# The second expert product with one 80-column stationary operand per chunk in place of a 64-column and a 16-column one

## The chip, the cores and the metric

The kernel runs on one core of one Trainium2 chip. The metric is device time in microseconds, the median of several executions. TensorE (PE, and PEld for its weight loads), VectorE (DVE), ScalarE (ACT) and GpSimd (POOL) each take their instructions in order; SyncE (SP) issues the large transfers.

## What is computed

A gated recurrence over 4 sequences of 5056 steps and 256 channels, then a mixture of 8 experts on the 20224 resulting rows. Each row goes to the expert with the largest logit, and each expert keeps the 80 rows with the largest gate; all other output rows are zero.

```python
for t in range(S):
    h = f[:, t] * h + i[:, t] * x[:, t]
    y[:, t] = h
...
for e in range(E):
    ...
    h = np.maximum(x[tok_idx] @ w1[e], 0.0)
    out[tok_idx] = gate_w[tok_idx, None] * (h @ w2[e])
```

`w1[e]` is 256 x 1024, `w2[e]` is 1024 x 256, all in fp32.

## The kernel before

The first part computes the recurrence in transposed form (channels on partitions) into `h_all`, 40 units of 512 steps, and the gate logits; then a ranking stage finds the 80 rows of each expert. The last part, `experts`, is where the change lies.

Per expert e it has these steps. `gather(e)` (L719) copies 80 columns of `h_all` into X(e), 24 on VectorE, 32 on ScalarE and 24 on GpSimd, each of which first loads the column numbers into registers; `scaled(e)` (L730) multiplies X(e) on GpSimd. `hidden(e)` (L736), the first product, called h(e) below, multiplies the 80 rows by `w1[e]`: the stationary operand is a piece of 64 columns of `w1`, the moving one is X(e) with 80 columns, and two pieces go to the two halves of the PSUM partitions. `relu(e)` (L753) rectifies the lower half of the 1024 hidden channels on ScalarE and the upper half on VectorE, into HID(e), eight chunks of 128 channels x 80 rows. `result(e)` (L757), the second product, called y(e) below, goes over the eight chunks: HID is stationary, `w2` moves with 256 columns, and the 80 rows are cut into two pieces, rows 0 to 63 and rows 64 to 79. `finish(e)` (L767) multiplies by the gates on VectorE, and `scatter(e)` (L773) writes the 80 rows to the output by an indirect transfer of GpSimd.

The order is written out by hand: h(0), h(1), then for each e the rectification of e, h(e+1) if it is still to come, the gather of e+3, y(e), the finish of e. So TensorE runs h(0), h(1), y(0), h(2), y(1), h(3), ..., h(7), y(6), y(7), with seven warm-up matmuls (L160, 128 stationary columns, 512 moving) around h(0) and h(1). After y(0) VectorE works out the output rows of all experts (L834 to L837, `rows_of`) before its half of relu(1).

The weights come in halves of 512 KB: two per `w1[e]` and two per `w2[e]`, in the list `w1[0]`, `w1[1]`, `w2[0]`, `w1[2]`, `w2[1]`, `w1[3]`, `w2[2]`, `w1[4]`, `w2[3]`, `w1[5]`, `w2[4]` and so on (L505). Seven slots hold them in turn, so half k can be loaded when TensorE is through with half k - 7. SyncE issues them in this order; between them it issues copies that clear parts of the output (`copied`, L131, 512 KB each, the last one 256 KB), after the halves with the numbers in

```python
BETWEEN = (7, 8, 8, 10, 12, 13, 15, 16, 18)
```

(L526). Of the list's numbers, 11 is the second half of `w1[3]`, 12 the first half of `w2[2]` and 20 the first half of `w2[4]`. A DMA queue of SyncE has eight semaphores, and a transfer waits until the one eight before it has landed.

The scatters of experts 2 to 6 wait for a mark on TensorE, a given chunk of a given second product (`apart`, L814; for expert 6 it is chunk 6 of y(7)), and the scatter of expert 7 waits until all others have landed.

Of the kernel before, what the change touches and what calls it, by code (L numbers as in the profile page):

```python
# [26 lines left out]
def kernel(  # L27
# [11 lines left out]
    nc = tc.nc  # L39
# [4 lines left out]
    FC = F // P  # L44
# [5 lines left out]
    K = (capacity + TOP - 1) // TOP * TOP  # L50
# [20 lines left out]
    FH, CH = F // 2, FC // 2  # L71
# [90 lines left out]
    with tc.tile_pool(name="gsm", bufs=1) as gsm:  # L162
# [239 lines left out]
        with tc.tile_pool(name="plg", bufs=1, space=PSUM) as plg, \  # L402
# [48 lines left out]
            with tc.tile_pool(name="pct", bufs=4, space=PSUM) as pct:  # L451
                cts = {}

                def turn(*runs):
                    ct = pct.tile([P, 4 * P], F32, name="ct", tag="ct")
                    for g0, g1 in runs:
                        turned(ct[:, ds((g0 - runs[0][0]) * P, (g1 - g0) * P)], g0, g1)
                        cts[g0] = ct, runs[0][0]
                    return ct
# [24 lines left out]
                c = turn((6, LAST - 1), (LAST - 1, LAST))  # L484
# [113 lines left out]
    with tc.tile_pool(name="sel", bufs=1) as sel, \  # L598
# [17 lines left out]
        for r in (rivals2, rivals):  # L616
            nc.tensor.matmul(r, mates, spread.rearrange("p c k -> p (c k)"),
                             start=True, stop=True)
# [89 lines left out]
    def experts(again):  # L708
        with tc.tile_pool(name="xp", bufs=3) as xp, \
# [7 lines left out]
            sent, marks = [], {}  # L717
# [16 lines left out]
            H = P // 2  # L734
# [22 lines left out]
            def result(e):  # L757
                halves = [w.pop((2, e, i)) for i in range(2)]
                hid = HID.pop(e)
                y = Y[e] = psy.tile([K, D], F32, name="y_ps", tag="y_ps")  # L760
                for c in range(FC):
                    for s0, n in ((0, H), (H, K - H)):
                        marks[e, c] = nc.tensor.matmul(  # L763
                            y[ds(s0, n)], hid[:, c, ds(s0, n)], halves[c // CH][:, c % CH],
                            start=c == 0, stop=c == FC - 1, skip_group_check=True)

            def finish(e):  # L767
                if e == 0:
# [47 lines left out]
            for e in range(E):  # L816
                relu(e, ps)
                if e == 0 and not again:
                    gates_of(slots[:, 1])
                if e + 1 < E:  # L820
                    ps = hidden(e + 1)
                    more(1)
                if e == E - 4:
                    scatter(0)
                if e + 3 < E:
                    gather(e + 3)
                    scaled(e + 3)
                if e == E - 4:
                    scatter(1)
                result(e)  # L830
                more(1)
                finish(e)
                if e == 0 and not again:
                    found = consts.tile([1, 1], F32, name="found")  # L834
                    nc.vector.tensor_reduce(found, total, AX.X, ALU.add)
                    nc.vector.tensor_copy(doubt, found)
                    rows_of(consts, slots[:, 0], slots[:, 1])  # L837
# [94 lines left out]
```

## Time and profile before

| | us |
|---|---|
| median of 3 runs (252.64 to 252.92) | 252.69 |
| the profiled execution | 253.41 |
| its span, first to last instruction | 251.5 |
| TensorE busy, of that span | 221.4 (88%) |
| VectorE, ScalarE, GpSimd busy | 156.8, 133.1, 143.2 |

Times in the trace count from the start of the span. A busy matmul record is a pipelined one: records overlap, and the distance between the starts of two records tells the cost of the first. An fp32 matmul stands in the trace as two records, each with a weight load of its own.

### The profile page before, as it was taken

The page shows a single profiled execution, that of the slowest core. Times are in us where ns is not written, and L with a number is a line of the kernel's source. Part 1 is how long each engine was busy: PE and PEld are TensorE (multiplying, and loading weights), DVE is VectorE, ACT ScalarE, POOL GpSimd, SP SyncE. Part 2 cuts the span into 40 slices and gives each one's busy share as a digit, 9 for nine tenths or more (in the row PEclk, how much of TensorE's full clock was granted, in tenths as well). Part 3 has the DMA queues.
Part 4 walks back from the last instruction along what each step waited for, and adds up shares of the span by engine and source line. Part 5 has one row for each costly group of instructions (what it writes and reads, how often), then busy time and mean ns, then how long its engine had stood idle before and what let it go on. Part 6 is the DMA issues. An engine that isn't in the chain of part 4 may idle for free.

```text
span 251.5 us, 6853 instructions
## 1 busy us (share of the span) xinstructions
PE 221.4 (88%) x2223; PEld 141.9 (56%) x2223; DVE 156.8 (62%) x400; ACT 133.1 (53%) x419; POOL 143.2 (57%) x287
## 2 busy tenths in 40 slices
PE   0699899899989998999966899799999999999960
PEld 0698787778868787777834646252525344352210
DVE  4189699999999999899999567435415051010100
ACT  4488798779787886888826066755042300000000
POOL 4678797889788798779844067650450620011211
PEclk9999999999999999999997979999999999999996
DMA  6999999999999999999999999969985474620000
GB/s 248 377 410 449 371 425 412 418 420 401 412 405 408 397 434 391 395 403 412 400 363 417 416 444 402 417 257 345 340 300 199 154 250 137 219 95 14 26 20 17
DMA packets 21363, 80.61 MB, mean 320 GB/s; under 512 B 2580, under 2 KB 2710, under 8 KB 20888
## 3 DMA queue, kind: packets, MB, share of 16 engines
q1 hardware_dynamic: 20936, 79.45, 80.4%
q0 software_dynamic: 384, 0.66, 0.9%
q8 instruction: 19, 0.31, 0.5%
q14 instruction: 24, 0.20, 0.2%
HBM read 72.62 MB, written 21.36 MB: 374 GB/s over the span
## 4 chain that ended last, share of the span: by engine, by line
PE 45%; issue 19%; ACT 10%; DVE 9%; DMA 9%; POOL 4%; ACTq 1%; DVEq 0%; POOLq 0%; SPq 0%
PE y_ps L763 14%; PE sp L251 11%; PE up L259 9%; PE lg L289 6%; DMA x_t<-in_x_dram 5%; ACT h_all L268 4%; ACT xe L727 3%; PE h_ps L747 3%; DMA f_t<-in_f_logit_dram 3%; DVE h_all L276 3%; POOL out_dram L775 2%; PE lt L313 2%; POOL x_t L245 2%; ACT ls L298 2%; DMA out_dram<-y,goal 1%
## 5 line engine op out<-in xcount | busy, mean ns | idle before, releaser
L245 POOL TENSOR_TENSOR x_t<-f_t,x_t 128x1024 f32<-128x1024 f32 x40 | 94.7, 2370 | 21.1 <-DMA x_t<-in_x_dram 10.6
L276 DVE TENSOR_TENSOR_SCAN h_all<-h_all,up 128x512 f32<-128x512 f32 (+1 forms) x80 | 95.8, 1244 | 9.9 <-PE up L259 6.4
L763 PE MATMUL y_ps<-w_sb,hid 128*64 128x256 f32 (+1 forms) x256 | 71.3, 393 | 1.4 <-ACT hid L754 1.4
L268 ACT ACTIVATE h_all<-sp,nomlb 128x512 f32<-128x512 f32 (+1 forms) x80 | 50.3, 677 | 16.5 <-PE sp L251 15.7
L763 PEld LDWEIGHTS y_ps<-w_sb,hid 128*64 128x64 f32 (+1 forms) x256 | 19.4, 115 | 50.4 <-issue 48.8
L241 ACT ACTIVATE f_t<-f_t 128x1024 f32<-128x1024 f32 x40 | 42.3, 1058 | 9.8 <-DMA f_t<-in_f_logit_dram 7.3
L259 PE MATMUL up<-ident,x_t 128*128 128x128 f32 x320 | 44.0, 278 | 2.8 <-DVE h_all L276 2.2
L251 PE MATMUL sp<-ident,f_t 128*128 128x128 f32 x320 | 45.4, 287 | 0.0
L251 PEld LDWEIGHTS sp<-ident,f_t 128*128 128x128 f32 x320 | 35.9, 145 | 7.8 <-issue 7.1
L259 PEld LDWEIGHTS up<-ident,x_t 128*128 128x128 f32 x320 | 36.7, 143 | 5.1 <-DVE h_all L276 3.7
L771 DVE TENSOR_SCALAR y<-y_ps,gates 80x256 f32<-80x256 f32 x8 | 3.8, 480 | 57.0 <-PE y_ps L763 51.5
L727 ACT COPY xe<-h_all 128x2 f32 x256 | 25.4, 190 | 18.8 <-issue 12.2
L727 POOL COPY xe<-h_all 128x2 f32 x192 | 24.3, 189 | 14.2 <-issue 7.0
L727 DVE COPY xe<-h_all 128x2 f32 x192 | 22.7, 173 | 12.0 <-issue 7.4
L775 POOL DMA_INDIRECT out_dram<-y,goal x8 | 7.5, 942 | 35.3 <-PE y_ps L763 31.1
L289 PE MATMUL lg<-h_all,wg 128*32 128x128 f32 (+1 forms) x640 | 26.4, 282 | 0.6 <-ACT ls L298 0.6
L754 ACT ACTIVATE hid<-h_ps 128x320 f32<-128x320 f32 x8 | 3.5, 435 | 39.2 <-PE h_ps L747 21.3
L747 PEld LDWEIGHTS h_ps<-xe,w_sb 128*64 128x64 f32 x512 | 18.2, 138 | 4.1 <-issue 3.6
L747 PE MATMUL h_ps<-xe,w_sb 128*64 128x80 f32 x512 | 19.5, 234 | 0.0
L289 PEld LDWEIGHTS lg<-h_all,wg 128*32 128x32 f32 x640 | 15.4, 108 | 7.0 <-issue 4.9
L731 POOL TENSOR_TENSOR xe<-xe,omlb 128x160 f32<-128x160 f32 x8 | 3.6, 452 | 23.5 <-DVE xe L727 22.1
L160 PE MATMUL warm<-h_all,ident 128*128 128x512 f32 x22 | 13.1, 740 | 0.0
(128 smaller groups left out, 105.6 us busy)
## 6 DMA issues: line engine op xcount, KB each, us to landing
f_t<-in_f_logit_dram SPq DMA_DIRECT2D x40, 512.0 KB, 6.6
x_t<-in_x_dram SPq DMA_DIRECT2D x40, 512.0 KB, 6.9
w_sb<-in_moe_w_dram SPq DMA_DIRECT2D x31, 512.0 KB, 5.0
out_dram<-out_dram SPq DMA_DIRECT2D x26, 512.0 KB, 8.2
out_dram<-zbuf SPq DMA_DIRECT2D x12, 512.0 KB, 10.0
out_dram<-h_all SPq DMA_DIRECT2D x1, 512.0 KB, 8.2
w_sb<-in_moe_w_dram SPq DMA_DIRECT2D x2, 256.0 KB, 2.8
out_dram<-out_dram SPq DMA_DIRECT2D x1, 256.0 KB
```

The lines of the kernel that those rows point to most:

```text
L160: nc.tensor.matmul(warm, ident, h_all[:, 0, :4 * P], start=True, stop=True)
L241: nc.scalar.activation(s_t, s_t, ACT.Sigmoid, scale=-1.0)
L245: nc.gpsimd.tensor_tensor(u_t, sts[n], u_t, ALU.mult)
L251: nc.tensor.transpose(ps[:, ds(r * P, P)], sts[n][:, r, ds(o * P, P)], ident)
L259: nc.tensor.transpose(ps[:, r::R], uts[n][:, r, ds(o * P, P)], ident)
L268: nc.scalar.activation(columns(n, o).rearrange("p (k r) -> p k r", r=R), sps.pop((n, o)).rearrange("p (r k) -> p k r", r=R)[:, P - run(n / ...
L276: nc.vector.tensor_tensor_scan(h, h, ups.pop((n, o)), h_all[:, o, ds(spot(n - B) + G - 1, 1)] if n >= B else 0.0, ALU.mult, ALU.add)
L289: nc.tensor.matmul(lgs[g][ds(q * LC, LC), b, :k].rearrange("p (m i) -> p m i", i=2), wg[:, o], pairs[:, :, q], start=o == 0, stop=o == DC ...
L727: copy(X[e][:, :, ds(k + j, 1)], h_all[:, :, ds(v, 1)])
L747: nc.tensor.matmul(ps[i][ds(s * H, H), c], wo[o][:, at:at + J * (H - 1) + 1:J], xt[:, o], start=o == 0 and c == 0, stop=o == DC - 1, skip_ ...
L763: marks[e, c] = nc.tensor.matmul(y[ds(s0, n)], hid[:, c, ds(s0, n)], halves[c // CH][:, c % CH], start=c == 0, stop=c == FC - 1, skip_grou ...
L775: sent.append(nc.gpsimd.indirect_dma_start(out=out, out_offset=bass.IndirectOffsetOnAxis(ap=goal[:, ds(e, 1)], axis=0), in_=rows.pop(e), i ...
```

## The change

`result` runs one matmul per chunk, with all 80 columns of the chunk of HID as the stationary operand, and writes the whole `y` tile with it. The mark of a chunk is that matmul.

```diff
@@ -759,10 +759,9 @@
                 hid = HID.pop(e)
                 y = Y[e] = psy.tile([K, D], F32, name="y_ps", tag="y_ps")
                 for c in range(FC):
-                    for s0, n in ((0, H), (H, K - H)):
-                        marks[e, c] = nc.tensor.matmul(
-                            y[ds(s0, n)], hid[:, c, ds(s0, n)], halves[c // CH][:, c % CH],
-                            start=c == 0, stop=c == FC - 1, skip_group_check=True)
+                    marks[e, c] = nc.tensor.matmul(
+                        y, hid[:, c], halves[c // CH][:, c % CH],
+                        start=c == 0, stop=c == FC - 1, skip_group_check=True)
```

On TensorE, from the end of h(1) through y(0) to h(2), the program before has, with the waits of each instruction (DMAHW is a landing of weights; the sizes are stationary columns x moving columns):

```order
L747 MATMUL h_ps<-xe,w_sb 64x80 x15
L763 MATMUL y_ps<-w_sb,hid 64x256 [waits DMAHW2_49,Activation_49]
L763 MATMUL y_ps<-w_sb,hid 16x256
L763 MATMUL y_ps<-w_sb,hid 64x256
L763 MATMUL y_ps<-w_sb,hid 16x256
```

The row pair of 64 and 16 goes on to the eighth chunk, and the fifth chunk's first row waits for the second half of the weights and for VectorE. The changed program has there:

```order
L747 MATMUL h_ps<-xe,w_sb 64x80 x15
L762 MATMUL y_ps<-w_sb,hid 80x256 [waits DMAHW2_49,Activation_49]
L762 MATMUL y_ps<-w_sb,hid 80x256 x3
L762 MATMUL y_ps<-w_sb,hid 80x256 [waits DMAHW4_49,DVE_49]
L762 MATMUL y_ps<-w_sb,hid 80x256 x3
L747 MATMUL h_ps<-xe,w_sb 64x80 [waits DMAHW6_49,PE_49,Pool_49]
```

The waits stand at the same two places, chunks 0 and 4. On the other engines the program's rows are the same as before but for line numbers, which are one lower behind L763.

## Rows read from the trace of the kernel before

**Rows 1.** The chain that ended last, by engine and line, shares of the span.

```profile
PE y_ps L763 14%; PE sp L251 11%; PE up L259 9%; PE lg L289 6%; DMA x_t<-in_x_dram 5%; ACT h_all L268 4%; ACT xe L727 3%; PE h_ps L747 3%; DMA f_t<-in_f_logit_dram 3%; DVE h_all L276 3%; POOL out_dram L775 2%; PE lt L313 2%; POOL x_t L245 2%; ACT ls L298 2%; DMA out_dram<-y,goal 1%
```

**Rows 2.** Busy time by stretch, with its header: the second products.

```profile
core 0: us, PE busy (x) PEld busy (x) DVE busy (x) ACT busy (x) POOL busy (x), PEclk, DMA share, GB/s
158.50:242.80 84.30, 84.30 (x640) 32.62 (x640) 22.28 (x148) 18.87 (x167) 23.86 (x133) 1.00 0.55 198
```

**Rows 3.** TensorE in order of time: start, length, instructions, idle time before.

```profile
149.49 2.44 PE L747 MATMUL h_ps<-xe,w_sb 128*64 128x80 f32 x64
...
158.49 8.96 PE L763 MATMUL y_ps<-w_sb,hid 128*64 128x256 f32 x32 [1.43 <-ACT hid L754]
167.39 2.44 PE L747 MATMUL h_ps<-xe,w_sb 128*64 128x80 f32 x64
169.65 8.91 PE L763 MATMUL y_ps<-w_sb,hid 128*64 128x256 f32 x32
178.50 2.44 PE L747 MATMUL h_ps<-xe,w_sb 128*64 128x80 f32 x64
...
225.21 17.80 PE L763 MATMUL y_ps<-w_sb,hid 128*64 128x256 f32 x64
```

**Rows 4.** Weight loads in order of time, inside y(1).

```profile
170.18 0.11 PEld L763 LDWEIGHTS y_ps<-w_sb,hid 128*16 128x16 f32 x2 [0.39 <-issue]
170.71 0.19 PEld L763 LDWEIGHTS y_ps<-w_sb,hid 128*64 128x64 f32 x2 [0.42 <-issue]
171.29 0.11 PEld L763 LDWEIGHTS y_ps<-w_sb,hid 128*16 128x16 f32 x2 [0.38 <-issue]
```

**Rows 5.** TensorE in order of time: the second pass of y(1)'s first piece.

```profile
169.87 0.38 PE L763 MATMUL y_ps<-w_sb,hid 128*64 128x256 f32 x1
```

**Rows 6.** Weight loads in order of time: the warm-up's last, then h(0).

```profile
148.11 0.19 PEld L160 LDWEIGHTS warm<-h_all,ident 128*128 128x128 f32 x1 [0.24 <-issue]
148.54 0.19 PEld L160 LDWEIGHTS warm<-h_all,ident 128*128 128x128 f32 x1 [0.24 <-issue]
149.48 0.14 PEld L747 LDWEIGHTS h_ps<-xe,w_sb 128*64 128x64 f32 x2 [0.76 <-issue]
```

**Rows 7.** Weight loads in order of time: the warm-up that follows h(0).

```profile
151.85 0.30 PEld L160 LDWEIGHTS warm<-h_all,ident 128*128 128x128 f32 x2
152.39 0.19 PEld L160 LDWEIGHTS warm<-h_all,ident 128*128 128x128 f32 x1 [0.24 <-issue]
```

**Rows 8.** SyncE's issues in order of time.

```profile
157.50 0.52 SPq L137 DMA_DIRECT2D out_dram<-out_dram  x1
163.04 0.34 SPq L514 DMA_DIRECT2D w_sb<-in_moe_w_dram  x1
```

**Rows 9.** Line 137 in the stretch around 157.5: the one copy issued there.

```profile
DMA to landing us min/median/max: 10.2/10.2/10.2
```

**Rows 10.** Busy time by stretch (columns as in rows 2).

```profile
127.00:133.00 6.00, 3.28 (x28) 1.99 (x24) 5.62 (x20) 1.90 (x6) 1.52 (x3) 1.00 0.98 372
133.00:139.00 6.00, 5.00 (x10) 2.74 (x10) 5.79 (x20) 3.72 (x15) 3.29 (x13) 0.72 1.03 416
147.70:149.40 1.70, 1.70 (x5) 0.55 (x3) 0.17 (x1) 0.23 (x3) 0.45 (x1) 0.99 1.15 471
133.00:163.00 30.00, 26.80 (x259) 15.66 (x260) 20.80 (x136) 16.38 (x142) 16.89 (x112) 0.89 1.03 418
```

**Rows 11.** ScalarE in order of time: relu(0), gather(3), relu(1).

```profile
158.01 0.43 ACT L754 ACTIVATE hid<-h_ps 128x320 f32<-128x320 f32 x1
160.03 3.34 ACT L727 COPY xe<-h_all 128x2 f32 x32 [1.59 <-issue]
163.27 0.43 ACT L754 ACTIVATE hid<-h_ps 128x320 f32<-128x320 f32 x1
```

**Rows 12.** VectorE in order of time: its half of relu(1).

```profile
170.13 0.48 DVE L755 TENSOR_SCALAR hid<-h_ps 128x320 f32<-128x320 f32 x1
```

**Rows 13.** GpSimd in order of time: the scatters of experts 6 and 7.

```profile
242.18 0.91 POOL L775 DMA_INDIRECT out_dram<-y,goal  x1 [4.65 <-PE y_ps L763]
246.12 0.91 POOL L775 DMA_INDIRECT out_dram<-y,goal  x1 [3.03 <-DMA out_dram<-y,goal]
```

## The prediction

> **What bounds the kernel now.** I read the chain of waits first: it ends through the second product, whose line 763 is its largest single entry, 14% of the span [rows 1]. The busy table by stretch comes next. From the first second product to the last, 84.3 us, TensorE is busy the whole time at a granted clock of 1.00, while the DMA engines are at 0.55 [rows 2]. So this stage, a third of the span, is paced by TensorE and nothing else, and what the change saves there is saved on the path until something else is late. TensorE's own order shows the cycle: y(0) starts at 158.49, h(2) at 167.39, y(1) at 169.65, h(3) at 178.50 [rows 3]. An expert costs 2.26 us of first product and 8.85 to 8.90 us of second product.
>
> The weight loads inside one second product show why the latter is so long. A load of 16 columns starts at 170.18, one of 64 at 170.71, one of 16 again at 171.29 [rows 4]. Each piece has two records (an fp32 matmul has two passes here), and the two pieces of a chunk follow one another: 0.53 + 0.58 = 1.11 us a chunk, eight of them 8.9. Inside a piece the second pass starts 0.215 us after the first (169.65, then 169.87) [rows 3, 5]. So of 1.11 us, 4 x 0.215 = 0.86 is streaming 256 columns four times, and 0.25 goes into the two changes of side, before each of which the load row shows 0.38 to 0.42 us of waiting [rows 4].
>
> **The change, part by part.** All of it is on TensorE. Per expert 16 matmuls (32 records) become 8 (16 records), each with 80 stationary columns and the same 256 moving ones.
>
> *A pass.* No row has 80 columns in an fp32 stationary against 256 moving. The nearest are the warm-up matmuls, 128 columns against 512: load follows load by 0.43 us (148.11, 148.54) at a granted clock of 0.99 [rows 6, 10]. That is 2 x 0.215, so 512 columns cost just twice the 256 of rows 5, and the load of the next stationary adds nothing: it runs beside the pass before. I take 0.215 a pass. The other bound is a load that isn't hidden: on the first warm-up matmul after another shape, 0.54 us lie between the passes instead of 0.43 [rows 7], so 128 columns cost 0.11, 80 columns 80/128 of it, 0.07. I take it once per second product, and sixteen times for the upper bound. The Trainium skill speaks for that bound ("TensorE: Matmul & The Clock Gate", "What overlaps and what doesn't"): a weight load overlaps a running matmul only where the row groups differ, and here they are the same. By it this sum would lose 16 x 8 x 0.07 us; the warm-up rows speak against it.
>
> *Leaving a second product.* From the last warm-up load at 148.54 the next shape's load starts at 149.48 [rows 6]: one pass of 0.43 lies between them, so the last pass begins at 148.97 and 0.51 later the next shape loads, 0.43 of streaming plus 0.08. For 256 columns I take 0.215 + 0.09 = 0.31, which is what the change of side costs today, so nothing is added.
>
> *Entering it.* Today h(e+1) and the 64-column piece have the same column width, and h to y takes 2.26. The first product of expert 0 was followed by a 128-column matmul, and there 149.49 to 151.85 is 2.36 [rows 3, 7]. So 0.10 is added at six entries (y(1) to y(6)).
>
> *Sum on TensorE.* y before h: 0.28 + 14 x 0.215 + 0.31 = 3.60 instead of 8.85, 5.25 less, six times: 31.5, plus 0.05 because y(0) took 8.90. y(6) and y(7) follow each other: 17.80 us [rows 3] become 0.28 + 30 x 0.215 + 0.38 (a record's length) = 7.11: 10.7 less. Minus 6 x 0.10. Together **41.6 us**, with a cycle of 3.60 + 2.26 + 0.10 = 5.96 us per expert instead of 11.11.
>
> *Who can follow at 5.96.* ScalarE's gather is the longest: from one rectification at 158.01 to the next at 163.27 it needs 5.26 with the 32 copies in between [rows 11]. That fits, and X(e+3) is wanted three cycles later. VectorE's half of relu(1) started 2.74 us after h(2) (167.39, 170.13), behind the row arithmetic [rows 3, 12]. Now h(2) starts at 162.1, so it ends near 165.3; the fifth chunk of y(1) wants it at 162.1 + 2.36 + 0.28 + 7 x 0.215 = 166.2. Not late, by 0.9.
>
> *The weights can't follow.* They come in halves of 512 KB through seven slots, on one queue, with zero copies of the same size between them. In 133 to 163 the queue moved 418 GB/s at a DMA share of 1.03 [rows 10]: 1.25 us for 512 KB. The copy issued at 157.50 landed 10.2 us later [rows 8, 9], at 167.7. Today the next half is issued at 163.04 [rows 8], when y(0) has used its first half, and the queue then drains. After the change that half is issued at 160.3, and from there each issue comes before the queue is empty. Behind the copy stand, by the program's list up to the first half of w2[4]: 10 halves and 4.5 copies, 14.5 x 1.25 = 18.1, so that half lands at 185.8. TensorE would want it at 158.49 + 4 x 5.96 = 182.3. **It is 3.5 us late**, spread over h(4), y(3) and h(5). After it no copies are left; four halves take 5.0 us, less than a cycle, and the rest of the weights is in time. Bounds: 0, if TensorE's wants are a little later than I say; 5.5, at 1.40 us for 512 KB.
>
> *The tail.* The row scatter of expert 6 waits for chunk 6 of y(7); the last scatter waits until that one has landed (242.18, then 246.12) [rows 13]. The mark was 1.11 us before the end of y(7) and is now 0.43. The tail after TensorE grows by **0.7**.
>
> 41.6 - 3.5 - 0.7 = 37.4. The profiled execution took 253.41 us, 216.0 after the change; it stood 0.7 above the median of the runs, 252.69. That gives **215.3 us**.
>
> **The rivals.**
> *Weights in time* (0.15). The queue is never really the last: 3.5 us come back, 211.8. For it: the margin is a fifth of a cycle per expert. Against it: the 10.2 us landing.
> *Weights later still, or a slow clock behind them* (0.17). At 1.40 us per half the wait is 14.5 x 0.15 = 2.2 longer; or TensorE's gaps cost it the clock: after a stretch with 3.28 of 6 us busy the granted clock in the next 6 us was 0.72 [rows 10], some 2 us of work lost. Against: the 1.43 us gap before y(0) [rows 3] left the clock at 1.00 [rows 2]. About 217.5, both together 219.5.
> *Loads not hidden* (0.05). 15 x 0.07 more per second product is 8.4 us on TensorE; the cycle is then 7.0, the half of w2[4] is wanted at 186.5, after it lands, and the 3.5 are not paid: 215.3 + 8.4 - 3.5 = 220.2.
> *The pieces overlap already* (0.02). Then TensorE streams a chunk's two pieces at once, joining them saves nothing, and the time stays within 0.2% of 252.7. The Trainium skill ("TensorEngine Tiling (Array Packing)", "Key Properties") says that different tiles load and multiply in parallel, which for two column pieces would be this case. The trace has it for the first product (64 records of 80 columns in 2.26 us, 0.035 each, half of 0.215 x 80/256) but not here, where 1.11 us a chunk are more than both pieces in a row. The same section says that a change of tiling mode drains TensorE, and 64 and 16 columns are two modes.
> *Slower* (0.01). The 80-column matmuls run like the first warm-up ones of a cold stretch, at half clock and with the load on top. It decides if a pass takes over 8.9/16 = 0.55 us. Half clock gives 0.43; with a load uncovered at the lengthiest row for one, 0.19 us at full clock [rows 6] and so 0.38, 0.81: 16 x 0.81 = 13.0 against 8.9, eight times 4.1 more, about 285. The granted clock of 1.00 through the whole stage [rows 2] speaks against it.
>
> **How the numbers follow.** The forecast has 0.60. The range takes in the first two rivals but not both mishaps of the second together: 211.5 to 218.5. A measurement of this kernel can tell 0.2% from no change; all cases but two are faster by more, so faster 0.97, same 0.02, slower 0.01.
>
> **What would show it.** Right: 256 y records become 128, 0.215 us apart, with one load wait per second product where there were 16; y to h in 3.6, h to y in 2.36; gaps of TensorE in front of h(4), y(3) and the middle of y(3) that end with a landing of w_sb, 3 to 4 us in all, and none from y(4) on; DMA share near 1.0 until about 185. Wrong: passes 0.28 apart (loads not hidden); no gap at all (weights in time); a granted clock under 1.00 between 165 and 200; or gaps on TensorE that end with xe (the gathers).

## The result, and the profile after

The changed kernel took 216.53 us in the median of 4 runs (216.16 to 216.97), the kernel before on the same chip 252.81 us: a ratio of 0.8562 [0.8537, 0.8588]. The prediction was 215.3 us with a range of 211.5 to 218.5, so it holds, 1.2 us too low. The profiled execution took 216.18 us against the 216.0 of the prediction's sum, with a span of 214.3 us. One execution of later and one of spread_tail (its profiled one) were in a slower state, so the ratios below leave these two out, the medians do not, and the trace of spread_tail is not used for times.

First the page of the changed kernel: busy times, the DMA share in 40 slices, and the second product's group of matmuls.

```profile
PE 180.3 (84%) x2095; PEld 142.1 (66%) x2095; DVE 156.6 (73%) x400; ACT 132.4 (62%) x419; POOL 143.9 (67%) x287
...
DMA  6999999999999999999999999999999999999110
...
L762 PE MATMUL y_ps<-w_sb,hid 128*80 128x256 f32 x128 | 29.5, 382 | 3.3 <-DMA w_sb<-in_moe_w_dram 2.9
```

TensorE is 41 us less busy (221.4 before), and the work of all other engines is what it was. The second product is 128 records instead of 256. The DMA engines, at 0.55 through the second products before [rows 2], are now full to within 16 us of the end. The chain that ended last no longer lists the second product, 14% of the span before [rows 1], among its entries. From the first second product on it goes through two of the zero copies, a load of weights, GpSimd's gather of the last expert and the scatters. TensorE is still in it: between the scatters GpSimd waits for marks on TensorE (4.98 us for L762 before the scatter at 196.18). This is the chain in order of time (start, length):

```profile
157.99 9.38 DMA out_dram<-out_dram
167.38 10.60 DMA out_dram<-out_dram
178.04 5.91 DMA w_sb<-in_moe_w_dram
...
205.18 3.01 DMA out_dram<-y,goal
```

TensorE in order of time shows the new cycle and what interrupts it. These rows answer to [rows 3]; the last column is idle time and what ended it.

```profile
157.94 3.68 PE L762 MATMUL y_ps<-w_sb,hid 128*80 128x256 f32 x16 [0.39 <-ACT hid L754]
161.55 2.44 PE L747 MATMUL h_ps<-xe,w_sb 128*64 128x80 f32 x64
163.92 3.68 PE L762 MATMUL y_ps<-w_sb,hid 128*80 128x256 f32 x16
167.53 2.44 PE L747 MATMUL h_ps<-xe,w_sb 128*64 128x80 f32 x64
...
172.60 1.93 PE L762 MATMUL y_ps<-w_sb,hid 128*80 128x256 f32 x8 [0.71 <-DMA w_sb<-in_moe_w_dram]
175.24 2.49 PE L747 MATMUL h_ps<-xe,w_sb 128*64 128x80 f32 x64 [0.71 <-DMA w_sb<-in_moe_w_dram]
179.35 1.93 PE L762 MATMUL y_ps<-w_sb,hid 128*80 128x256 f32 x8 [1.62 <-DMA w_sb<-in_moe_w_dram]
181.88 1.93 PE L762 MATMUL y_ps<-w_sb,hid 128*80 128x256 f32 x8 [0.60 <-DMA w_sb<-in_moe_w_dram]
...
186.27 3.65 PE L762 MATMUL y_ps<-w_sb,hid 128*80 128x256 f32 x16
...
198.20 7.13 PE L762 MATMUL y_ps<-w_sb,hid 128*80 128x256 f32 x32
```

Undisturbed, y to h takes 3.61 us (157.94 to 161.55), h to y 2.37, and a cycle 5.98 (157.94 to 163.92), instead of 8.85 to 8.90, 2.26 and 11.11. Four times TensorE waits for weights, 3.64 us in all, in the middle of y(2), before h(4), before y(3) and in its middle. From y(4) on it doesn't wait again.

The busy table by stretch (columns as in [rows 2]) says who is the slow one:

```profile
163.00:181.00 18.00, 14.96 (x198) 11.14 (x193) 12.21 (x86) 11.14 (x106) 11.02 (x76) 1.00 1.01 407
187.00:193.00 6.00, 6.00 (x82) 4.62 (x81) 2.44 (x16) 0.44 (x1) 3.79 (x22) 1.00 1.00 379
193.00:199.00 6.00, 6.00 (x82) 4.62 (x81) 0.88 (x2) 0.44 (x1) 0.91 (x1) 1.00 0.94 354
```

While TensorE is 14.96 of 18 us busy, the DMA engines are busy throughout, at 407 GB/s. The granted clock is 1.00 in spite of the waits. The queue stays full to about 199.

### The profile page after: what moved, and what is told of

Read it like the earlier page. It is cut to its first block, busy times and chain, and to the rows that moved or that the text cites. A ratio compares the mean times of both kernels' runs of the same rounds, so it can differ in the third digit from the quotient of the medians.

```text
span 214.3 us, 6597 instructions
## 1 busy us (share of the span) xinstructions
PE 180.3 (84%) x2095; PEld 142.1 (66%) x2095; DVE 156.6 (73%) x400; ACT 132.4 (62%) x419; POOL 143.9 (67%) x287
## 4 chain that ended last, share of the span: by engine, by line
PE 42%; DMA 22%; ACT 10%; issue 9%; DVE 9%; POOL 4%; POOLq 1%; SPq 1%; DVEq 0%; ACTq 0%
PE sp L251 13%; PE up L259 10%; DMA out_dram<-out_dram 9%; PE lg L289 7%; ACT h_all L268 6%; DMA f_t<-in_f_logit_dram 5%; PE warm L160 4%; DVE h_all L276 3%; PE lt L313 3%; DMA w_sb<-in_moe_w_dram 3%; DMA h_all<-in_moe_w_gate_dram 3%; POOL out_dram L774 2%; PE h_ps L747 2%; ACT ls L298 2%; PE slots L684 2%
## 5 line engine op out<-in xcount | busy, mean ns | idle before, releaser
L259 PEld LDWEIGHTS up<-ident,x_t 128*128 128x128 f32 x320 | 37.3, 144 | 3.4 <-DVE h_all L276 3.3
L762 PE MATMUL y_ps<-w_sb,hid 128*80 128x256 f32 x128 | 29.5, 382 | 3.3 <-DMA w_sb<-in_moe_w_dram 2.9
L762 PEld LDWEIGHTS y_ps<-w_sb,hid 128*80 128x80 f32 x128 | 18.5, 150 | 12.2 <-ACT hid L754 2.3
L160 PE MATMUL warm<-h_all,ident 128*128 128x512 f32 x22 | 12.5, 713 | 0.0
L313 PE MATMUL lt<-ident,ls 128*128 128x128 f32 (+1 forms) x40 | 7.4, 309 | 4.4 <-ACT ls L298 4.4
```

The costliest lines, as they stand in the source:

```text
L160: nc.tensor.matmul(warm, ident, h_all[:, 0, :4 * P], start=True, stop=True)
L259: nc.tensor.transpose(ps[:, r::R], uts[n][:, r, ds(o * P, P)], ident)
L313: nc.tensor.transpose(lts[g0][:k, g - g0, j], ls[:, j::R], ident)
L762: marks[e, c] = nc.tensor.matmul(y, hid[:, c], halves[c // CH][:, c % CH], start=c == 0, stop=c == FC - 1, skip_group_check=True)
```

## The experiments

Two kernels ask why the old pieces were slow, two leave the last zero copies out or move them, and the others build on that. The ratio is to the kernel before on the same chip; a kernel that ran once has none.

| run | us (runs) | ratio |
|---|---|---|
| the change | 216.53 (4) | 0.8562 [0.8537, 0.8588] |
| again, the change on another chip | 217.25 (4) | 0.8544 [0.8491, 0.8597] |
| wide64, two pieces of 64 columns | 219.13 (4) | 0.8635 [0.8587, 0.8683] |
| three32, pieces of 32, 32, 16 | 218.7 (1) | |
| nocopy, nocopy2, five copies left out | 212.64 (1), 213.31 (4) | 0.8403 [0.8372, 0.8435] |
| later, five copies at the end | 218.39 (4) | 0.8551 [0.8468, 0.8633] |
| tail, tail2, earlier marks for scatters | 215.37 (4), 215.18 (6) | 0.8464 [0.8426, 0.8501], 0.8464 [0.8433, 0.8496] |
| spread_tail, spread_tail2, copies spread too | 215.01 (4), 214.53 (6) | 0.8423 [0.8365, 0.8482], 0.8444 [0.8417, 0.8470] |
| all3, spread_tail with two pieces of 64 | 217.26 (4) | 0.8545 [0.8508, 0.8581] |

### Pieces of equal width: wide64

The 80 rows in two pieces again, but both 64 columns wide; the second has 16 real columns and 48 that are not used. HID of both parities lies in one tile, so that the 48 columns can be read past a chunk's end; GpSimd zeroes part of this tile first, and a scratch tile of the row arithmetic was moved to make room. The second product itself (the other pieces of the edit are left out):

```diff
-                    marks[e, c] = nc.tensor.matmul(
-                        y, hid[:, c], halves[c // CH][:, c % CH],
-                        start=c == 0, stop=c == FC - 1, skip_group_check=True)
+                    for s0 in (0, H):
+                        marks[e, c] = nc.tensor.matmul(
+                            y[ds(s0, H)], both[:, ds((e % 2 * FC + c) * K + s0, H)],
+                            halves[c // CH][:, c % CH],
+                            start=c == 0, stop=c == FC - 1, skip_group_check=True)
```

> Two pieces again, but both 64 columns wide (the second one holds rows 64 to 79 and 48 columns of no use). Theory (the old pieces followed one another because 64 and 16 are two column widths): the pieces now overlap like those of the first product. y to h 3.4 to 3.5 us, h to y 2.26 (no change of shape on either side, 0.2 less per expert than with 80 columns). The weights still set the pace up to y(4), so only y(4) to y(7) gain: about 0.8 us less than the change, 215.5. Rival (two column pieces with 256 moving columns follow one another whatever their widths): y stays at 7 us or more per expert, time 238 to 253.

Measured: 219.13 us. TensorE in order of time, wide64:

```profile
160.37 3.67 PE L767 MATMUL y_ps<-w_sb,hid 128*64 128x256 f32 x32 [2.11 <-ACT hid L757]
163.87 2.38 PE L750 MATMUL h_ps<-xe,w_sb 128*64 128x80 f32 x64
166.08 3.62 PE L767 MATMUL y_ps<-w_sb,hid 128*64 128x256 f32 x32
...
188.67 3.67 PE L767 MATMUL y_ps<-w_sb,hid 128*64 128x256 f32 x32
...
204.44 3.67 PE L767 MATMUL y_ps<-w_sb,hid 128*64 128x256 f32 x32 [0.59 <-ACT hid L757]
```

The same 32 records as before the change, with more columns in them, now take 3.50 us (160.37 to 163.87) instead of 8.9. Two pieces of 64 columns run side by side, so the old pieces were slow because 16 columns stood beside 64, and not because there were two. The cycle is 5.71 us, 0.27 shorter than with 80 columns, since h and y now are of one width (h to y 2.21). Nothing of that reaches the end: y(4) starts 28.30 us after y(0), and after the change 28.33, because the weights pace this stretch. The time missed its expectation of 215.5 on two other counts. The unused columns of y(6) lie in HID(7), so relu(7) on ScalarE has to wait for the end of y(6) (it starts at 203.95, after y_ps), and y(7) waits for it in turn (0.59 us). And y(0) starts 1.8 us later than in the run again (158.60). Part of that lies in the edit: ScalarE begins the gather of expert 0 1.8 us after the end of `slots` (144.86 to 146.64), in tail 0.7 us after it (144.80 to 145.51), and y(0) waits for ScalarE. all3, the other kernel with the zeroing, has the same delay (144.45 to 146.11). Whether the zeroing (0.67 us here, 0.14 there) or another piece of the edit brings it about was not settled.

### Pieces of 32, 32 and 16: three32

```diff
+                    for s0, n in ((0, 32), (32, 32), (64, K - 64)):
+                        marks[e, c] = nc.tensor.matmul(
+                            y[ds(s0, n)], hid[:, c, ds(s0, n)], halves[c // CH][:, c % CH],
+                            start=c == 0, stop=c == FC - 1, skip_group_check=True)
```

> Three pieces of 32, 32 and 16 columns, no padding. Theory (equal widths overlap; if a piece of 16 counts as one of 32): the three run side by side, y to h 3.5 to 3.7 us, time within 1 us of the change. Rival 1 (16 columns are a width of their own): two sides a chunk as before, 8.5 us or more per y, 250. Rival 2 (pieces never overlap here): three in a row, 8 x 6 x 0.215 = 10.3 and the changes of side, over 260.

Measured: 218.7 us in a single run. TensorE in order of time, three32:

```profile
159.36 3.65 PE L763 MATMUL y_ps<-w_sb,hid 128*32 128x256 f32 x48 [1.74 <-ACT hid L754]
162.94 2.44 PE L747 MATMUL h_ps<-xe,w_sb 128*64 128x80 f32 x64
165.31 3.65 PE L763 MATMUL y_ps<-w_sb,hid 128*32 128x256 f32 x48
```

48 records take 3.58 us, as long as the 16 of the change, and the cycle is 5.95. So the three pieces run side by side, and a piece of 16 columns goes along with those of 32. What made a chunk cost 1.11 us before was 64 beside 16. The time, expected within 1 us of the change, is 2.2 us above it in this one run; in the traces y(0) starts 1.4 us later than in the change (157.94). The Trainium skill ("TensorEngine Tiling (Array Packing)", "Key Properties") has both halves of this: tiles work in parallel, and a change of tiling mode drains TensorE. The two runs (0.44 and 0.45 us a chunk) and [rows 4] (1.11) agree with it; a drain as such stands in no row.

### Without the last copies: nocopy, nocopy2

The five copies are left out, so a part of the output is not cleared.

```diff
-    BETWEEN = (7, 8, 8, 10, 12, 13, 15, 16, 18)
+    BETWEEN = (7, 8, 8, 10)
```

> The change without the five copies behind halves 12, 13, 15, 16 and 18 (that part of the output is not cleared). Theory (the copies make the weights late): the four gaps of TensorE between y(2) and y(4), 3.6 us as idle time and 4.4 us as lateness of y(4), go; y(4) starts 4 x 5.98 after y(0); about 211.8. Rival (the weights are late by the slots and the time to landing, not by the bytes): gaps of over 2 us remain, 214 or more.

> The kernel of run nocopy once more, timed in rounds, on the chip of tail2 (the last five zero copies are left out, so that part of the output isn't cleared). Theory (the copies cost the change 4.4 us): 4 to 5 us less than the change has beside the kernel before (0.8544 and 0.8562), a ratio of 0.836 to 0.840. Rival (weights alone would have been late too): a ratio of 0.850 or more.

Measured: 212.64 us in a single run, and 213.31 as the median of four. TensorE in order of time, nocopy:

```profile
158.68 3.68 PE L762 MATMUL y_ps<-w_sb,hid 128*80 128x256 f32 x16 [1.51 <-ACT hid L754]
...
182.60 3.68 PE L762 MATMUL y_ps<-w_sb,hid 128*80 128x256 f32 x16
...
194.58 7.13 PE L762 MATMUL y_ps<-w_sb,hid 128*80 128x256 f32 x32
```

No row between them has a wait. y(4) comes 23.92 us after y(0), four cycles of 5.98, where the change took 28.33: the copies cost the change 4.4 us. In the ratios it is 0.8562 - 0.8403 = 0.0159 (0.0141 from the other chip's 0.8544), 4.0 us (3.6) of 253.9, with intervals that don't touch. That is 0.4 to 0.8 us less than the trace gives, and the ratio 0.8403 lies at the upper edge of what the theory gave. The rival, weights late by themselves, falls.

### Copies at the end: later

```diff
-    BETWEEN = (7, 8, 8, 10, 12, 13, 15, 16, 18)
+    BETWEEN = (7, 8, 8, 10, 24, 24, 24, 24, 24)
...
-                if e == E - 4:
-                    scatter(0)
                 if e + 3 < E:
                     gather(e + 3)
                     scaled(e + 3)
                 if e == E - 4:
+                    scatter(0)
                     scatter(1)
```

> The change with the same five copies behind half 24 instead, and the scatter of expert 0 behind the gather of expert 7. Theory (the bytes up to half 20 are what is late, and afterwards the queue has room): y(4) comes 4 us earlier, later weights are still in time, 212.3. Rival (the queue is full to the end, the wait only moves): gaps of the same 3 to 4 us in front of y(5) to y(7), 215.5 to 217.

Measured: 218.39 us, no gain. TensorE in order of time, later:

```profile
160.17 3.68 PE L762 MATMUL y_ps<-w_sb,hid 128*80 128x256 f32 x16 [0.82 <-ACT hid L754]
...
184.09 3.68 PE L762 MATMUL y_ps<-w_sb,hid 128*80 128x256 f32 x16
...
194.85 3.39 PE L762 MATMUL y_ps<-w_sb,hid 128*80 128x256 f32 x8 [2.83 <-DMA w_sb<-in_moe_w_dram]
...
200.53 7.13 PE L762 MATMUL y_ps<-w_sb,hid 128*80 128x256 f32 x32
```

The busy table by stretch, where that wait ends, later:

```profile
193.00:199.00 6.00, 4.15 (x32) 2.69 (x34) 0.73 (x2) 0.00 (x0) 2.53 (x3) 0.72 1.03 362
```

y(4) is 23.92 us after y(0), as without copies, and then all five copies stand before one half of y(5): one wait of 2.83 us, and behind it half a y that takes 3.39 us instead of 1.93 in a stretch with a granted clock of 0.72. From y(0) to the end of y(7) it is 47.49 us (160.17 to 207.66), in the change 47.39. The wait only moved, as the rival said, and brought a clock loss of 1.46 us with it. The median lies above the rival's 215.5 to 217 too; in the trace y(0) starts 2.2 us later than in the change (last section).

### The tail, and copies spread: tail, spread_tail, and again

The run again is the change itself, as a yardstick for the other chip. tail lets the scatters of experts 4 to 6 go earlier in TensorE's order; spread_tail takes this and puts the five copies one by one behind later halves, with scatter(0) moved as in later.

```diff
-            apart = {2: (E - 3, FC - 1), 3: (E - 2, 0), 4: (E - 2, FC - 1), 5: (E - 1, 1),
-                     6: (E - 1, FC - 2)}
+            apart = {2: (E - 3, FC - 1), 3: (E - 2, 0), 4: (E - 2, FC - 5), 5: (E - 2, FC - 1),
+                     6: (E - 1, 2)}
...
-    BETWEEN = (7, 8, 8, 10, 12, 13, 15, 16, 18)
+    BETWEEN = (7, 8, 8, 10, 13, 17, 20, 23, 26)
```

The first piece is tail; both together, with the move of scatter(0), are spread_tail.

> The changed kernel itself once more, on the chip of the three below: 216 to 218, ratio 0.856.

> The change with earlier marks for three scatters: expert 4 behind chunk 3 of y(6), expert 5 behind y(6), expert 6 behind chunk 2 of y(7). Theory (the chain behind TensorE goes through the scatter of expert 6, its landing and the scatter of expert 7): the scatter of expert 6 starts some 1.7 us earlier and the last one 1.7 to 2 us earlier, limited by the finish of y(7); 2 us less than the change. Rival (the last scatter waits for something else, VectorE or the branch): under 0.5 us less.

> The marks of tail, and the five copies behind halves 13, 17, 20, 23 and 26, one per expert, with the scatters of experts 0 and 1 behind the gather of expert 7. The bytes stay the same. Theory (the queue is full nearly to the end, so the copies can be moved but not hidden): gaps of under 1 us each spread over y(2) to y(6), together 2.5 to 3.5 instead of 4.4; 1 to 1.5 us less than tail. Rival (the room behind half 20 is enough for them): no gaps, 4 us less than tail.

> The kernel of run tail once more, as the yardstick for spread_tail2 on one chip. Both theories: 0.846 of the kernel before, about 215 us.

> The kernel of run spread_tail once more, beside tail2. Theory (the copies only have to be out of the way at the moments when TensorE is about to run out of weights; spreading them takes away some of the four waits): 1 to 1.5 us less than tail2, a ratio near 0.841, waits on w_sb between y(0) and y(7) of 2 us or less in all instead of 3.6. Rival (the queue is full to the end, so a copy moved back delays a later half by as much): same time as tail2 within 0.3 us, the waits add up to the same 3.6 and stand in y(4) to y(6).

Measured: again 217.25, tail 215.37, tail2 215.18, spread_tail 215.01, spread_tail2 214.53 us. The last two scatters on GpSimd, first again, then tail (as in [rows 13]):

```profile
205.81 0.92 POOL L774 DMA_INDIRECT out_dram<-y,goal  x1 [0.88 <-PE y_ps L762]
209.89 0.92 POOL L774 DMA_INDIRECT out_dram<-y,goal  x1 [3.17 <-DVEq L845]
```

```profile
203.49 0.91 POOL L774 DMA_INDIRECT out_dram<-y,goal  x1 [0.38 <-PE y_ps L762]
207.69 0.91 POOL L774 DMA_INDIRECT out_dram<-y,goal  x1 [3.29 <-DMA out_dram<-y,goal]
```

TensorE ended at 205.96 in again and 205.36 in tail, so the last scatter goes 3.93 us after it in the one and 2.33 in the other, and the tail is 1.2 us shorter (spans of 215.3 and 213.5). By the medians tail gains 1.9 us, and every run of tail (214.96 to 215.73) lies below every run of again on that chip (216.29 to 218.55); the intervals of the two ratios still overlap by 0.001 (0.8426 to 0.8501 and 0.8491 to 0.8597). Not all of it is the tail: y(0) to the end of y(7) takes 46.12 us in tail, 47.36 in again. With the five copies spread, TensorE reads (in order of time, spread_tail2):

```profile
160.39 3.68 PE L762 MATMUL y_ps<-w_sb,hid 128*80 128x256 f32 x16 [1.00 <-ACT hid L754]
...
186.45 1.93 PE L762 MATMUL y_ps<-w_sb,hid 128*80 128x256 f32 x8 [0.19 <-DMA w_sb<-in_moe_w_dram]
...
191.51 3.65 PE L762 MATMUL y_ps<-w_sb,hid 128*80 128x256 f32 x16 [0.77 <-DMA w_sb<-in_moe_w_dram]
...
198.47 7.12 PE L762 MATMUL y_ps<-w_sb,hid 128*80 128x256 f32 x32 [0.31 <-issue]
```

Two waits for weights are left, 0.96 us together, and y(0) to the end of y(7) takes 45.20 us; tail2 takes 46.90 (158.88 to 205.78), tail, the same kernel, 46.12, and nocopy 43.03. So in the traces 0.9 to 1.7 us come back, about the 1 to 1.5 expected, and neither all 4 us, as the rival of spread_tail had it, nor nothing, as the rival of spread_tail2 had it. The move of the copies and that of scatter(0) were not tried apart. In the measured times no gain is shown: by the medians tail to spread_tail is 0.36 us and tail2 to spread_tail2 0.65, both less than expected, and the intervals overlap. In part this is the start: in the two profiled executions of tail2 and spread_tail2 y(0) starts 1.5 us later in spread_tail2, for a reason that lies before it (last section). spread_tail and spread_tail2, one kernel, have the lowest ratios of those that clear the whole output; the interval of 0.8417 to 0.8470 lies below both of the change's, so this version beats the change and the kernel before.

### Everything together: all3

spread_tail with the second product of wide64; the two parities of HID are swapped in their tile, so that y(7) isn't tied to another rectification (the other pieces of the edit are left out).

```diff
-                HID[e] = mp.tile([P, FC, K], F32, name="hid", tag="hid")
+                HID[e] = both[:, ds((1 - e % 2) * FC * K, FC * K)].rearrange("p (c k) -> p c k", k=K)
```

> spread_tail with the two 64-column pieces, and HID laid out so that the unused columns never belong to the next expert of y(7). Theory: TensorE needs 5.71 per expert instead of 5.98, but the weights pace it; 0.3 to 0.8 us less than spread_tail, and no wait for ScalarE between y(6) and y(7). Rival (TensorE still paces it): 2 us less.

Measured: 217.26 us, slower than spread_tail, a miss. TensorE in order of time, all3:

```profile
192.44 3.67 PE L767 MATMUL y_ps<-w_sb,hid 128*64 128x256 f32 x32 [1.23 <-DMA w_sb<-in_moe_w_dram]
...
198.29 8.33 PE L767 MATMUL y_ps<-w_sb,hid 128*64 128x256 f32 x64
```

The wait before y(7) is gone, but y(6) and y(7) take 8.33 us instead of the 7.13 of one 80-column piece, and TensorE waits longer for weights (1.23 us here, 2.70 in four waits, against 0.96 in spread_tail2). The 1.2 us more lie at the start of y(6): between 198.26 and 201.07 its weight loads stand idle four times, 1.3 us in all, and the profile shows nothing that they wait for; the granted clock is 1.00, and the other 48 loads follow without a gap. What held them was not settled. As built, two pieces of 64 columns are no gain over one of 80; but both kernels carry the late gather of expert 0, so the pieces alone were not compared.

## Why the prediction was right, and where it was off

The profiled executions, term by term:

| term | predicted | measured |
|---|---|---|
| TensorE, y(0) to the end of y(7), without waits for weights | -41.6 | -41.5 (84.52 to 43.0) |
| weights late | +3.5 | +4.4 (28.33 - 23.92) |
| tail behind TensorE | +0.7 | +0.5 (8.49 to 8.97) |
| start of y(0) | 0 | -0.55 (158.49 to 157.94) |
| sum | -37.4 | -37.2 (253.41 to 216.18) |

43.0 is the changed kernel's 47.39 (157.94 to 205.33) less the 4.4.

*A pass at 0.215, loads hidden.* Right. Weight loads of the changed kernel in order of time:

```profile
163.92 3.24 PEld L762 LDWEIGHTS y_ps<-w_sb,hid 128*80 128x80 f32 x16
```

Sixteen loads of 80 columns lie within 3.24 us, some 0.21 apart, and y to h is 3.61 us where the sum had 3.60; loads that aren't hidden would have made it 4.65. The Trainium skill has a load overlap a running matmul only in another row group ("TensorE: Matmul & The Clock Gate", "What overlaps and what doesn't"). By that rule the change would have cost 8.4 us more on TensorE; the trace does not bear it out here, as all loads go to the same 128 rows and are hidden all the same.

*Leaving and entering.* Right: h to y is 2.37 (2.36), y(6) with y(7) 7.13 (7.11), the cycle 5.98 (5.96).

*Why pieces were slow.* The prediction gave 0.25 us of 1.11 to the changes of side. The runs wide64 and three32 show more: with equal widths the pieces of a chunk cost 0.44 us (3.50 in eight chunks), so 64 beside 16 cost the overlap too.

*Who can follow.* Right: ScalarE needs 5.25 us from one rectification to the next, and no wait of TensorE behind y(0) ends with a gather or with VectorE.

*The weights.* The mechanism was right; the term was sized too small. The copy that the sum starts from was issued at 157.99; these are its landing (line 137 around 157.99), and that of the first half of w2[4], issued at 176.42 (line 520):

```profile
DMA to landing us min/median/max: 9.4/9.4/9.4
```

```profile
DMA to landing us min/median/max: 9.7/9.7/9.7
```

From 167.4 to 186.1, 18.7 us for 14.5 transfers, 1.29 us for each where I took 1.25 from a stretch at 418 GB/s [rows 10]; this stretch has 407. The prediction's 185.8 for that half was 0.3 early, TensorE wanted it 0.4 earlier than said because y(0) was earlier (157.94 + 4 x 5.98 = 181.9), and y(4) starts 0.2 after it has landed: together the 0.9 between 3.5 and 4.4. In the details: a wait stands in the middle of y(2) that I didn't list and none before h(5); and the DMA share is 1.00 to 193 and 0.94 to 199, where I had it near 1.0 until about 185.

*The tail.* The term is right: the scatter of expert 6 went 0.83 us before TensorE's end and now goes 0.15 before it (205.18 against 205.33), 0.68 later. The tail as a whole grew by 0.5, as the steps behind this scatter took 0.2 less.

*From the sum to the median.* The profiled execution was met within 0.2 us, in part because the earlier start of y(0) offset the weights; it isn't the change's, as in again y(0) starts at 158.60. The rest of the 1.2 us is the correction of 0.7: the profiled execution stood 0.7 above its median before and stands 0.35 below it after.

Of the rivals, "weights in time" (211.8) is what nocopy shows with the copies gone, and "a slow clock behind them" came about in later and not in the change, whose longest wait was 1.62 us. "The pieces overlap already" fell for 64 with 16, but would have been right for 64 with 64.

## What to carry to other kernels

Be careful where a stationary operand is cut into column pieces: 64 beside 16 followed one another here, while 64 with 64, and 32 with 32 and 16, ran side by side (3.50 and 3.58 us per product, 3.61 for the one piece of 80). When an engine that paced a stage gets twice as fast, list what its transfers wait behind: here 14.5 transfers on one full queue took back 4.4 us of 41.5, and moving the five that nobody waits for to one place only made one long wait; spread out, they left shorter waits in the trace, though the gain in time is within the noise. With the bound gone, look at marks that were set for the old pace: here earlier marks for the scatters gained 1.9 us by the medians, more than spreading the copies.

## What was not expected of the hardware

*Weights alone fill the queue.* In nocopy the same stretch reads (busy table):

```profile
163.00:181.00 18.00, 18.00 (x249) 13.85 (x246) 13.00 (x93) 11.36 (x106) 11.25 (x78) 1.00 1.00 386
```

That is a DMA share of 1.00 with no wait of TensorE, so the share of the DMA engines alone doesn't tell whether weights are late.

*The length of one wait doesn't settle the clock.* One wait of 2.83 us was followed by a stretch at 0.72 (later), and the four waits of up to 1.62 us in the change left the granted clock at 1.00. In between there is no order: a wait of 2.14 us in tail2 left it at 1.00 (TensorE, then the busy table behind it),

```profile
179.83 1.93 PE L762 MATMUL y_ps<-w_sb,hid 128*80 128x256 f32 x8 [2.14 <-ACT hid L754]
```

```profile
179.80:186.00 6.20, 5.64 (x68) 4.09 (x70) 0.88 (x2) 3.22 (x32) 1.26 (x3) 1.00 1.03 410
```

while one of 2.09 us in the next paragraph was followed by 0.50. What else decides was not tried.

*A faster warm-up, and slow work behind it.* In the ranking stage six warm-up records run ahead of the matmuls of `slots`. TensorE in order of time, then the busy table from 140 to 144, of spread_tail2:

```profile
134.62 2.74 PE L160 MATMUL warm<-h_all,ident 128*128 128x512 f32 x6
139.44 0.49 PE L671 MATMUL sums_p<-count,before 128*128 128x1 f32 x2 [2.09 <-DVE taken L668]
...
142.38 4.16 PE L684 MATMUL slots<-what,put 128*80 128x8 bf16 x60
```

```profile
140.00:144.00 4.00, 3.82 (x50) 3.67 (x51) 2.29 (x13) 0.00 (x0) 0.00 (x0) 0.50 1.02 416
```

The same two views of tail2:

```profile
135.12 4.39 PE L160 MATMUL warm<-h_all,ident 128*128 128x512 f32 x6
139.91 0.38 PE L671 MATMUL sums_p<-count,before 128*128 128x1 f32 x2 [0.40 <-DVE taken L668]
...
142.00 2.46 PE L684 MATMUL slots<-what,put 128*80 128x8 bf16 x60
```

```profile
140.00:144.00 4.00, 3.62 (x80) 3.46 (x81) 2.54 (x14) 0.00 (x0) 0.00 (x0) 1.00 1.03 417
```

In spread_tail2 the warm-up runs at the full clock, takes 2.74 us and leaves 2.09 idle; then the clock is granted at 0.50 (1.2 GHz) and `slots` takes 4.16 us instead of 2.46. In tail2 the warm-up itself runs slower and fills that time, and `slots` runs at 2.4 GHz. The start of y(0) differs by 1.5 us between the two, as much as the smaller edits above are worth. The slow `slots` stands in the profiles of later, spread_tail and spread_tail2 and in part in the change's own (3.36 us), each time behind a warm-up of 2.74 us; the other nine have a warm-up of 3.53 us or more and a `slots` of 2.46 to 2.57. No edit is needed for it: the change and again are one kernel, with 2.74 and 3.36 us in the one and 3.53 and 2.57 in the other. That the early end of the warm-up brings the slow `slots` about is not shown: the clock falls in all of these traces, in the nine already under the warm-up (0.67 from 134 to 137 in tail2, 1.00 in spread_tail2), and no run changed the warm-up alone.
